# A fused scan and two expert layers on one core: tail clears, scatters, a page table and two ranks moved to other slots

## The chip, the core and the metric

The kernel runs on one core of a Trainium2 chip. The metric is the device time of one execution in microseconds; three runs of the kernel before took 588.43, 592.61 and 591.45 us, median 591.45. The profile is of one further execution.

## The reference

Three layers, in float32. The first is a gated linear scan over 4 batches, 8 heads and 768 positions, the second a dense layer pair with a leaky activation, the third a layer of 8 experts of which each token uses one:

```python
y[:, :, sl] = y_intra + y_inter                  # scan by chunks: (C B^T * decay) x + C state * decay
x = y.transpose(0, 2, 1, 3).reshape(3072, 256)
h = x @ w_in                                     # 256 -> 2048
x = (np.maximum(h, 0) + alpha * np.minimum(h, 0)) @ w_out
logits = x @ w_gate + modality_bias[modality_id] # 8 experts
e_idx = np.argmax(logits, axis=1)
for e in range(8):                               # each token goes to one expert
    mask = e_idx == e
    out[mask] = gate_w[mask, None] * (np.maximum(x[mask] @ w1[e], 0) @ w2[e])
```

## The kernel before, in words

**Blocks.** The 3072 tokens are 24 chunks of 128, grouped in nine blocks (`SIZES`: three of 2 chunks, six of 3). For each block the scan is computed, then the dense pair in 16 pieces of the hidden width. A piece is one *slot*: `unit_mm` multiplies into PSUM (`ph`), ScalarE and VectorE form the activation (`t`, `g`), `unit_split` splits it in a high part on ScalarE (`gh`) and a low part on GpSimd (`gl`, L618), and four slots later (`LAG`) `unit_g2` multiplies both by the second matrix into `px`. The scan of the next block runs in the same slots. Every matrix product is done in three matmuls on such high and low parts.

**Routing.** When a block is done, its tokens are routed: `route_mm` and `route_act` give the logits, `route_b` to `route_gate` the expert and its weight, `route_c` the ranks of the tokens within their expert (small matmuls into `pr`), `route_d` (L553) the row of each token in the DRAM buffer `srt`, and keeps the running count per expert in `cnt`. Still in `route_d`, one indirect DMA per chunk (L569), issued from GpSimd, scatters the 128 rows of the chunk to `srt`. In `srt` each expert has its own region, read later in pages of 256 rows.

**Clears.** An expert's last page is not full. `tail_counts` (L1012) copies `cnt` to integers (`cnti`, L1013), and `clear_tails` (L457) issues, from SyncE, one DMA per expert that writes 5 x 128 empty rows (645 KB) behind the counted ones. The rows of the last block are scattered after the clears, over them; the rows of the other blocks don't overlap them.

**Pages.** 14 pages of 256 rows follow, 8 slots each. For a page, SyncE reads the expert and the first row from a table (`item_tables`, computed on VectorE from `cnt` in five steps, one a slot: `sets`, `rk`, `knw`, `va`, `tab`). There are three: table 0 serves pages 0 and 1, table 1 pages 2 to 8, table 2 the rest. `item_load` (L771) loads 2 MB of the expert's weights in four DMAs (`raw`), `item_rows` (L786) the 256 rows (`xr`); the latter waits for all scatters and clears that stand before it in the program. `item_split` makes high and low weights on ScalarE and VectorE, `item_tr_mm` transposes the rows on TensorE (`pt`, L827), `item_tr_act` splits them (`x2h` on ScalarE, `x2l` on VectorE, L837); `item_g1` and `item_g2` are the two matmul steps (`rh`, `rl`).

**The order.** From block 3 on the order on each engine is written by hand: 96 block slots, numbered 0 to 95 (blocks 3 to 8), then 112 page slots. `do(u, fn, ...)` puts a step behind the work of slot `u`; `at[k, f]` is the slot of piece `f` of block `k`, so `at[8, 11]` is slot 91, and `ui` is slot 96. Within a slot the steps stand in the order of the `do` calls. Each engine takes its instructions in order. Block 7 is routed up to slot 90 and block 8 up to slot 106. Pages 0 and 1 are loaded at slots 83 and 84, page 2 at slot 96.

Of the kernel before, what the change touches and what calls it, by code (L numbers as in the profile page):

```python
# [112 lines left out]
def ssm_moe_moe_kernel(  # L113
# [26 lines left out]
    blocks = [(sum(SIZES[:k]), n) for k, n in enumerate(SIZES)]  # L140
# [57 lines left out]
    blk = {}  # L198
# [160 lines left out]
    m2p = []  # L359
# [187 lines left out]
    scat, tails = [], []  # L547

    def wait_for(i, o, why):
        tc.add_manual_dep(i, o.name, mybir.DependencyInfo(mybir.DependencyClass.Sync, mybir.DependencyReason.DATA),  # L550
                          reason=why)

    def route_d(k):  # L553
        c0, n = blocks[k]
        d = blk[k]
        pr, oh, xr = d["pr"], d["oh"], d["xr"]
        sh = [P, n, NE]
        V = nc.vector

        q = small.tile([P, MX, NE], F32, tag="q", name="q")  # L560
        V.tensor_tensor(q[:, :n], pr[:, :n], cnt[:, None, :].to_broadcast(sh), ALU.add)
        V.tensor_tensor(cnt, pr[:, n], cnt, ALU.add)
        V.tensor_tensor(q[:, :n], q[:, :n], oh[:, :n], ALU.mult)
        pf = small.tile([P, MX], F32, tag="pf", name="pf")
        V.tensor_reduce(pf[:, :n], q[:, :n], AX.X, ALU.add)
        pi = small.tile([P, MX], I32, tag="pi", name="pi")
        V.tensor_copy(pi[:, :n], pf[:, :n])
        for t in range(n):
            sc = nc.gpsimd.indirect_dma_start(  # L569
                out=srt[:, :], out_offset=bass.IndirectOffsetOnAxis(ap=pi[:, t:t + 1].bitcast(U32), axis=0),  # L570
                in_=xr[:, t, :ROW], in_offset=None, bounds_check=NROW - 1, oob_is_err=False)

            for o in scat:
                tc.declare_no_dep(sc.ins, o, reason="rows are disjoint")
            scat.append(sc.ins)
            if k == len(blocks) - 1:
                for o in tails:
                    wait_for(sc.ins, o, "rows behind the last ones")
# [366 lines left out]
                nk += 1  # L945
    for step in (route_a, route_b, route_exp, route_gate, route_c, route_d):
        step(0)

    last = len(blocks) - 1
    slots = [("m",) + q for q in late] + [("i", i, fc) for i in range(NSTATIC) for fc in range(KF2)]
    at = {q[1:]: u for u, q in reversed(list(enumerate(slots))) if q[0] == "m"}
    ui = len(late)
# [3 lines left out]
    def do(u, fn, *args):  # L958
        todo.setdefault(u, []).append((fn, args))
# [65 lines left out]
    def route_at(k, mms, b):  # L1025
        for t, u in enumerate(mms):
            do(u, route_mm, k, t)
            do(u + 1, route_act, k, t)
        for v, fn in zip(b, (route_b, route_exp, route_gate, route_c, route_d)):
            do(v, fn, k)  # L1030

    u = at[NS, 0]
    route_at(1, (u, u + 1), (u + 4, u + 5, u + 6, u + 6, u + 8))
    route_at(2, (u + 5, u + 7), (u + 9, u + 10, u + 11, u + 11, u + 14))
    for k in range(NS, last + 1):
        u = at[k, 15] + 1
        if k < last - 1:
# [4 lines left out]
    def table_at(u, j, pool):  # L1042
        steps = []

        def step():
            if not steps:
                steps.append(item_tables(j, pool[-1]))
            next(steps[0], None)

        for v in range(u, u + 5):  # L1050
            do(v, step)

    table_at(at[last - 1, 14], 0, small_)
    table_at(at[last, 11], 1, m2p)
    do(ui, tail_counts)
    table_at(ui + 12, 2, m2p)

    for k in range(NS, last):
        c0, n = blocks[k + 1]
# [3 lines left out]
        for j in range(n):  # L1063
            c, b = c0 + j, at[k, 0] + 5 * j - (k > NS)
# [29 lines left out]
    for i in range(2, NSTATIC):  # L1094
        b = ui + KF2 * (i - 2)
# [109 lines left out]
```

## Time and profile before

| what | before |
| --- | --- |
| runs, us | 588.43, 592.61, 591.45 |
| profiled execution, us | 591.03 |
| its span, us | 589.2 |
| mean granted clock of TensorE | 0.956 |
| TensorE busy, us | 555.0 (94%) |
| VectorE, ScalarE, GpSimd busy, us | 431.7, 314.6, 238.6 |

TensorE is the engine with the most work, and 34 us of the span are not busy. The span's first 150 us hold the conversion of the weights and blocks 0 to 2, the block slots 0 to 95 lie from there to about 401 us, the pages behind. All times in rows are microseconds from the start of the span. PEclk is the granted TensorE clock as a share of 2.4 GHz.

### The profile page before, as it was taken

To read this page: it belongs to the slowest core of one execution; us is meant where nothing else is said; L and a number is where in the kernel's file an instruction comes from. 1 tells how busy PE (TensorE), PEld (TensorE's weight loads), DVE (VectorE), ACT (ScalarE), POOL (GpSimd) and SP (SyncE) were. 2 spreads that over 40 slices of the span, in tenths; PEclk is the share of its full clock that TensorE was granted. 3 is DMA by queue.
4 is the path that set the end of the run, shared out by engine and by line. 5 is a ranking of instruction groups with operands and counts; after the bars stand their busy time and mean duration, and the time that the engine had idled before them with its cause. 6 is when DMAs were issued, how large, how long until landed. Compare 5 with 4: busy or idle time off the path is not lost. (4 is left out here: it accounts for less than half of the span.)

```text
span 589.2 us, 12123 instructions
## 1 busy us (share of the span) xinstructions
PE 555.0 (94%) x4303; PEld 519.4 (88%) x4303; DVE 431.7 (73%) x857; ACT 314.6 (53%) x696; POOL 238.6 (41%) x258
## 2 busy tenths in 40 slices
PE   7989989998999989999999999997969999999993
PEld 7877878898988878999999999997969999999993
DVE  4999999834677877777677777487568778777860
ACT  1346756755443553444444444573546677767751
POOL 1144345554545635845746646453022122111211
PEclk9695999999799999999999999997979999999998
DMA  7856654420127335224243200721998877776400
GB/s 247 270 188 197 191 180 136 135 81 10 44 89 213 121 116 171 90 101 137 84 138 113 71 12 27 260 91 62 288 330 279 279 224 227 227 234 217 154 18 6
DMA packets 59124, 89.27 MB, mean 152 GB/s; under 512 B 5071, under 2 KB 37009, under 8 KB 59057
## 3 DMA queue, kind: packets, MB, share of 16 engines
q1 hardware_dynamic: 55942, 80.73, 43.4%
q0 software_dynamic: 2400, 6.32, 3.0%
q10 hardware_dynamic: 714, 1.38, 0.9%
q8 instruction: 36, 0.59, 0.4%
q14 instruction: 32, 0.25, 0.1%
HBM read 73.50 MB, written 15.17 MB: 150 GB/s over the span
## 5 line engine op out<-in xcount | busy, mean ns | idle before, releaser
L618 POOL TENSOR_TENSOR gl<-g,gh 128x384 fp32r<-128x384 f32 (+1 forms) x144 | 145.5, 1014 | 140.3 <-ACT gh L616 139.9
L607 ACT ACTIVATE t<-ph,sgn 128x384 f32<-128x384 f32 (+1 forms) x144 | 78.5, 545 | 120.5 <-PE ph L153 113.8
L609 DVE SCALAR_TENSOR_TENSOR g<-ph,sal,t 128x384 f32<-128x384 f32 (+1 forms) x144 | 81.3, 565 | 76.8 <-ACT t L607 69.7
L153 PE MATMUL ph<-xh,wi_h 128*128 128x384 f32 (+1 forms) x288 | 99.1, 346 | 2.3 <-DVE g L609 2.1
L153 PE MATMUL px<-gl,wo_h 128*128 128x384 f32 (+1 forms) x288 | 94.4, 328 | 2.3 <-POOL gl L618 2.2
L153 PE MATMUL px<-gh,wo_h 128*128 128x384 f32 (+1 forms) x288 | 93.8, 326 | 0.2 <-ACT xT L646 0.2
L153 PE MATMUL px<-gh,wo_l 128*128 128x384 f32 (+1 forms) x288 | 93.4, 325 | 0.3 <-DVE wo_l L159 0.3
L153 PE MATMUL ph<-xl,wi_h 128*128 128x384 f32 (+1 forms) x288 | 92.6, 322 | 0.0
L153 PE MATMUL ph<-xh,wi_l 128*128 128x384 f32 (+1 forms) x288 | 92.7, 322 | 0.0
L616 ACT CAST gh<-g 128x384 fp32r<-128x384 f32 (+1 forms) x144 | 67.6, 471 | 18.1 <-DVE g L609 17.6
L876 POOL DMA_INDIRECT out_dram<-ob,xr x26 | 27.9, 1071 | 112.1 <-ACT ob L875 62.5
L853 ACT ACTIVATE rh<-ph 128x256 fp32r<-128x256 f32 (+1 forms) x112 | 41.5, 371 | 54.3 <-PE ph L153 54.0
L854 DVE SCALAR_TENSOR_TENSOR rl<-ph,rh 128x256 fp32r<-128x256 f32 (+1 forms) x112 | 45.1, 403 | 23.3 <-ACT rh L853 22.4
L153 PEld LDWEIGHTS ph<-xh,wi_h 128*128 128x128 f32 x288 | 55.1, 193 | 7.4 <-DVE g L609 3.3
L153 PEld LDWEIGHTS px<-gl,wo_h 128*128 128x128 f32 x288 | 55.8, 194 | 4.0 <-POOL gl L618 2.7
L153 PEld LDWEIGHTS px<-gh,wo_h 128*128 128x128 f32 x288 | 55.8, 194 | 1.0 <-ACT xT L646 0.5
L153 PEld LDWEIGHTS px<-gh,wo_l 128*128 128x128 f32 x288 | 55.8, 194 | 0.7 <-DVE wo_l L159 0.5
L153 PEld LDWEIGHTS ph<-xl,wi_h 128*128 128x128 f32 x288 | 55.3, 192 | 0.4 <-DVE xl L159 0.3
L153 PEld LDWEIGHTS ph<-xh,wi_l 128*128 128x128 f32 x288 | 55.2, 192 | 0.2 <-DVE g L609 0.2
L153 PE MATMUL ph<-x2h,wi_h 128*128 128x256 f32 x144 | 41.8, 290 | 4.4 <-DVE rl L854 4.4
L964 DVE TENSOR_TENSOR_SCAN ab<-ab,id 128x512 f32<-128x512 f32 x30 | 44.2, 1475 | 0.0
L569 POOL DMA_INDIRECT srt<-xr,pi x24 | 25.7, 1072 | 42.0 <-DMA raw<-in_w_dram 29.0
(149 smaller groups left out, 1306.4 us busy)
## 6 DMA issues: line engine op xcount, KB each, us to landing
raw<-in_w_dram SPq DMA_DIRECT2D x56, 512.0 KB
ab<-a_scr SPq DMA_DIRECT2D x24, 512.0 KB
srt<-zr SPq DMA_DIRECT2D x8, 645.0 KB
raw<-in_w_in_dram SPq DMA_DIRECT2D x8, 512.0 KB
raw<-in_w_out_dram SPq DMA_DIRECT2D x8, 512.0 KB
xr<-srt SPq DMA_DIRECT2D x14, 258.0 KB
bs<-bcs SPq DMA_DIRECT2D x30, 96.0 KB
bs<-bcs SPq DMA_DIRECT2D x15, 192.0 KB
```

Of the source, the lines that this page charges most:

```text
L153: nc.tensor.matmul(o, l, r, start=start, stop=stop)
L569: sc = nc.gpsimd.indirect_dma_start(out=srt[:, :], out_offset=bass.IndirectOffsetOnAxis(ap=pi[:, t:t + 1].bitcast(U32), axis=0), in_=xr[:, ...
L607: nc.scalar.activation(t[:, :N], ph[:, :N], AF.Copy, scale=sg)
L609: nc.vector.scalar_tensor_tensor(g[:, :N], ph[:, :N], sal[:, fc:fc + 1], t[:, :N], ALU.mult, ALU.max)
L616: nc.scalar.copy(gh[:, :N], g[:, :N])
L618: nc.gpsimd.tensor_tensor(gl[:, :N], g[:, :N], f(gh[:, :N]), ALU.subtract)
L853: nc.scalar.activation(rh[:, :n], ph[:, :n], AF.Relu)
L854: nc.vector.scalar_tensor_tensor(rl[:, :n], ph[:, :n], 0.0, f(rh[:, :n]), ALU.max, ALU.subtract)
L876: nc.gpsimd.indirect_dma_start(out=out[:, :], out_offset=bass.IndirectOffsetOnAxis(ap=xr[:, t, ROW - 1:ROW].bitcast(U32), axis=0), in_=ob, ...
L964: nc.vector.tensor_tensor_scan(lt[:, s_].rearrange("p h i -> p (h i)"), lt[:, s_].rearrange("p h i -> p (h i)"), id8[:, s_].rearrange("p h ...
```

## The change

Five things move, and no computation is added or taken away. The scatters leave `route_d` and become a step of their own, `route_out`; for blocks 1 to 7 one chunk is scattered in each of the slots behind `route_d`, where two or three stood together. A scatter of a block before the last no longer depends on the clears, wherever it stands. The clears go from slot 96 to slot 91. Table 1 goes from slots 91 to 95 to slots 93 to 97. For blocks 1 and 2 the ranks (`route_c`) and `route_d` come one slot later.

```diff
--- before.py
+++ after.py
@@ -553,7 +553,7 @@
     def route_d(k):
         c0, n = blocks[k]
         d = blk[k]
-        pr, oh, xr = d["pr"], d["oh"], d["xr"]
+        pr, oh = d["pr"], d["oh"]
         sh = [P, n, NE]
         V = nc.vector
 
@@ -565,12 +565,16 @@
         V.tensor_reduce(pf[:, :n], q[:, :n], AX.X, ALU.add)
         pi = small.tile([P, MX], I32, tag="pi", name="pi")
         V.tensor_copy(pi[:, :n], pf[:, :n])
-        for t in range(n):
+        d["pi"] = pi
+
+    def route_out(k, ts):
+        pi, xr = blk[k]["pi"], blk[k]["xr"]
+        for t in ts:
             sc = nc.gpsimd.indirect_dma_start(
                 out=srt[:, :], out_offset=bass.IndirectOffsetOnAxis(ap=pi[:, t:t + 1].bitcast(U32), axis=0),
                 in_=xr[:, t, :ROW], in_offset=None, bounds_check=NROW - 1, oob_is_err=False)
 
-            for o in scat:
+            for o in scat + (tails if k < len(blocks) - 1 else []):
                 tc.declare_no_dep(sc.ins, o, reason="rows are disjoint")
             scat.append(sc.ins)
             if k == len(blocks) - 1:
@@ -945,6 +949,7 @@
                 nk += 1
     for step in (route_a, route_b, route_exp, route_gate, route_c, route_d):
         step(0)
+    route_out(0, range(blocks[0][1]))
 
 
 
@@ -1029,9 +1034,16 @@
         for v, fn in zip(b, (route_b, route_exp, route_gate, route_c, route_d)):
             do(v, fn, k)
 
+        n = blocks[k][1]
+        if k < last:
+            for t in range(n):
+                do(b[-1] + 1 + t, route_out, k, (t,))
+        else:
+            do(b[-1], route_out, k, range(n))
+
     u = at[NS, 0]
-    route_at(1, (u, u + 1), (u + 4, u + 5, u + 6, u + 6, u + 8))
-    route_at(2, (u + 5, u + 7), (u + 9, u + 10, u + 11, u + 11, u + 14))
+    route_at(1, (u, u + 1), (u + 4, u + 5, u + 6, u + 7, u + 9))
+    route_at(2, (u + 5, u + 7), (u + 9, u + 10, u + 11, u + 12, u + 15))
     for k in range(NS, last + 1):
         u = at[k, 15] + 1
         if k < last - 1:
@@ -1051,8 +1063,8 @@
             do(v, step)
 
     table_at(at[last - 1, 14], 0, small_)
-    table_at(at[last, 11], 1, m2p)
-    do(ui, tail_counts)
+    table_at(at[last, 13], 1, m2p)
+    do(at[last, 11], tail_counts)
     table_at(ui + 12, 2, m2p)
 
     for k in range(NS, last):
```

How the order on the engines moves is seen at two places. The first is VectorE at the end of the block slots. Before: `sets`, `rk`, `knw`, `va`, `tab` are table 1, `w2l` and `wi_l` the weights of pages 0 and 1, `x2l` page 0's rows, `rl` page 0's first slot.

```order
L734 TENSOR_TENSOR knw<-knw,rk 128x96
L159 TENSOR_TENSOR w2l<-raw_4982,w2h 128x512
L609 SCALAR_TENSOR_TENSOR g<-ph,sal,t 128x384
L737 SCALAR_TENSOR_TENSOR va<-rk,cst 128x192
L740 TENSOR_REDUCE tf<-va 128x2
L741 CAST tab_168<-tf 128x2
L837 TENSOR_TENSOR x2l<-pt,x2h 128x512
L609 SCALAR_TENSOR_TENSOR g<-ph,sal,t 128x384
L159 TENSOR_TENSOR wi_l<-raw_5032,wi_h 128x2x256
L854 SCALAR_TENSOR_TENSOR rl<-ph_5385,rh 128x256
L1013 CAST cnti<-cnt 128x8
```

The same place in the change, from the multiplication of `rk` in table 1 on:

```order
L728 TENSOR_TENSOR rk<-rk,sets 128x288
L731 TENSOR_TENSOR rk<-rk 128x96 x2
L841 TENSOR_TENSOR x2l<-pt,x2h 128x512
L613 SCALAR_TENSOR_TENSOR g<-ph,sal,t 128x384
L735 TENSOR_SCALAR knw<-rk 128x96
L737 TENSOR_SCALAR rk<-rk 128x96
L738 TENSOR_TENSOR knw<-knw,rk 128x96
L159 TENSOR_TENSOR wi_l<-raw_5032,wi_h 128x2x256
L858 SCALAR_TENSOR_TENSOR rl<-ph_5461,rh 128x256
L741 SCALAR_TENSOR_TENSOR va<-rk,cst 128x192
L744 TENSOR_REDUCE tf<-va 128x2
L745 CAST tab_168<-tf 128x2
```

And in the change a little earlier on VectorE, where the count of the clears stands now:

```order
L613 SCALAR_TENSOR_TENSOR g<-ph,sal,t 128x384
L1018 CAST cnti<-cnt 128x8
L159 TENSOR_TENSOR w2l<-raw_4980,w2h 128x512
L613 SCALAR_TENSOR_TENSOR g<-ph,sal,t 128x384
L159 TENSOR_TENSOR w2l<-raw_4982,w2h 128x512
L613 SCALAR_TENSOR_TENSOR g<-ph,sal,t 128x384
L698 SCALAR_TENSOR_TENSOR sets<-cnt,cst 128x96 x2
```

`cnti` stood behind the first `rl` of the pages and now stands five slots earlier, ahead of the table; the table's last three operations stood ahead of `x2l` and now stand behind the first `rl`.

The second place is GpSimd in the same slots, where the scatters of blocks 7 and 8 are issued. Before, block 7's, then block 8's:

```order
L618 TENSOR_TENSOR gl<-g,gh 128x384 x13
L569 DMA srt<-xr,pi 26880x258 x3
L618 TENSOR_TENSOR gl<-g,gh 128x384 x6
L569 DMA srt<-xr,pi 26880x258 x3
L876 DMA out_dram<-ob,xr_4984 3072x256 x2
```

In the change:

```order
L573 DMA srt<-xr,pi 26880x258
L622 TENSOR_TENSOR gl<-g,gh 128x384
L573 DMA srt<-xr,pi 26880x258
L622 TENSOR_TENSOR gl<-g,gh 128x384
L573 DMA srt<-xr,pi 26880x258
L622 TENSOR_TENSOR gl<-g,gh 128x384 x3
L573 DMA srt<-xr,pi 26880x258 x3
```

Block 7's three scatters have a `gl` between each two; block 8's three still stand together. On SyncE the sequence stays the same: eight clears, then page 2's weights and rows.

## Rows read from the trace of the kernel before

**Rows 1.** Waits of TensorE, whole run: us in total, times, longest.

```profile
PE ph L153 <- DVE rl L854: 4.4, 1, 4.4
...
PE ph L153 <- DVE x2l L837: 2.5, 1, 2.5
```

**Rows 2.** Stretches: us, busy PE, PEld, DVE, ACT, POOL (instructions), PEclk, DMA share, GB/s.

```profile
210.00:220.00 10.00, 7.88 (x47) 7.12 (x46) 7.27 (x13) 5.78 (x11) 3.46 (x4) 1.00 0.38 108
...
390.00:400.00 10.00, 10.00 (x68) 9.96 (x66) 9.69 (x21) 5.69 (x12) 7.38 (x7) 1.00 0.12 41
...
405.40:410.50 5.10, 5.06 (x19) 5.07 (x20) 2.69 (x5) 1.64 (x5) 1.01 (x1) 0.50 0.15 51
...
433.40:437.70 4.30, 3.64 (x16) 3.38 (x17) 4.13 (x17) 2.98 (x8) 0.00 (x0) 0.50 1.07 371
...
460.00:570.00 110.00, 110.00 (x939) 110.00 (x939) 85.29 (x161) 78.28 (x181) 22.51 (x21) 1.00 0.64 199
```

**Rows 3.** Timeline of TensorE, first gap: start, us, instruction, [idle before, releaser].

```profile
402.58 0.39 PE L153 MATMUL ph<-x2h,w1h 128*128 128x256 f32 x1 [1.23 <-ACT x2h L836]
...
405.44 0.58 PE L153 MATMUL ph<-x2l,w1h 128*128 128x256 f32 x1 [2.47 <-DVE x2l L837]
...
406.46 0.41 PE L153 MATMUL ph<-x2h,w1l 128*128 128x256 f32 x1
...
406.67 0.52 PE L153 MATMUL px<-gh,wo_h 128*128 128x384 f32 x1
...
411.90 0.28 PE L153 MATMUL ph<-x2h,w1l 128*128 128x256 f32 x1
...
412.01 0.34 PE L153 MATMUL px<-gh,wo_h 128*128 128x384 f32 x1
```

**Rows 4.** Timeline of VectorE around the first gap, and table 2.

```profile
392.71 0.61 DVE L609 SCALAR_TENSOR_TENSOR g<-ph,sal,t 128x384 f32<-128x384 f32 x1
...
396.07 3.71 DVE L724 TENSOR_TENSOR rk<-rk,sets 128x288 f32<-128x288 f32 x1
...
403.07 0.63 DVE L737 SCALAR_TENSOR_TENSOR va<-rk,cst 128x192 f32<-128x192 f32 x1
...
404.70 0.68 DVE L837 TENSOR_TENSOR x2l<-pt,x2h 128x512 fp32r<-128x512 f32 x1
...
407.73 0.17 DVE L1013 CAST cnti<-cnt 128x8 int32<-128x8 f32 x1
...
441.80 0.35 DVE L724 TENSOR_TENSOR rk<-rk,sets 128x192 f32<-128x192 f32 x1
```

**Rows 5.** Timeline of GpSimd: one undisturbed subtraction, then block 7's scatters and the pile.

```profile
371.95 1.02 POOL L618 TENSOR_TENSOR gl<-g,gh 128x384 fp32r<-128x384 f32 x1 [1.10 <-ACT gh L616]
...
392.47 1.19 POOL L569 DMA_INDIRECT srt<-xr,pi  x1 [1.29 <-DVE pi L567]
...
396.49 2.96 POOL L618 TENSOR_TENSOR gl<-g,gh 128x384 fp32r<-128x384 f32 x3
```

**Rows 6.** Timeline of TensorE, second gap, and the transposes of page 3.

```profile
433.49 0.58 PE L153 MATMUL ph<-x2h,wi_h 128*128 128x256 f32 x1 [4.43 <-DVE rl L854]
...
436.99 1.09 PE L827 MATMUL pt<-cst,xr 128*128 128x128 f32 x4 [0.57 <-DMA xr<-srt]
...
449.23 0.60 PE L827 MATMUL pt<-cst,xr 128*128 128x128 f32 x4
```

**Rows 7.** Timeline of ScalarE: the wait for page 2's weights.

```profile
431.75 0.62 ACT L815 CAST wi_h<-raw 128x512 fp32r<-128x512 f32 x1 [6.34 <-DMA raw<-in_w_dram]
```

**Rows 8.** Timeline of SyncE's issues: clears, weights of page 2, rows of pages 2, 3.

```profile
408.78 12.76 SPq L461 DMA_DIRECT2D srt<-zr  x8
...
423.06 2.92 SPq L783 DMA_DIRECT2D raw<-in_w_dram  x4
...
430.59 0.38 SPq L790 DMA_DIRECT2D xr<-srt  x1
...
443.77 0.38 SPq L790 DMA_DIRECT2D xr<-srt  x1
```

## The prediction

> **What bounds the kernel now.** I read the list of TensorE's waits first [rows 1]. The largest two of the late part are a wait of 4.4 us for `rl` and one of 2.5 us for `x2l`; both lie where the last block hands over to the expert pages. Then busy time and granted clock by stretches [rows 2]: TensorE is 10.00 of 10 busy at 1.00 in the block stage (390 to 400) and 110.00 of 110 in the page stage (460 to 570). A microsecond of TensorE's own work is therefore a microsecond of the kernel, and so is a gap of it; other engines matter where they make a gap. Two stretches stand out, 405.4 to 410.5 and 433.4 to 437.7, both at a granted clock of 0.50, the lower level (1.2 GHz), and each follows a gap.
>
> *First gap* [rows 3]. After the last block's matmuls TensorE idles 1.23 us for `x2h` and 2.47 us for `x2l`, and then runs at the lower clock: two 256-column matmuls start 0.21 us apart (406.46, 406.67), later 0.11 us (411.90, 412.01). Why is `x2l` late? VectorE [rows 4] spends 3.71 us (396.07) on one multiplication of 128x288 for table 1, where the same line took 0.35 us on 128x192 in table 2 (441.80). In just that time GpSimd [rows 5] runs three `gl` subtractions in one go (396.49, 2.96 us). They came in one go because the three scatters of block 7's rows, the first at 392.47, stood ahead of them in its queue until the pile began. So three scatters in a row piled up three `gl`, the pile held VectorE, and everything behind it there was late, `x2l` last.
>
> *Second gap* [rows 6]. TensorE idles 4.43 us at 433.49 and 0.57 us at 436.99 for page 2's gathered rows. ScalarE's row [rows 7] names the cause: it sat 6.34 us, until 431.75, for page 2's weights, and being in order could not produce the `rh` that TensorE needed. SyncE [rows 8] shows why they were late: eight tail clears (645 KB each) are issued from 408.78 for 12.76 us, and only then, at 423.06, the weights.
>
> **Part by part.** The sum is made against the profiled execution's own 591.03 us (span 589.2 and 1.8 around it); the median of the runs, 591.45, is 0.4 above.
>
> *Tails at slot 91 instead of 96.* `cnti` ran at 407.73 and the first clear 1.05 us later. In the new order `cnti` stands right behind the `g` that starts at 392.71 and lasts 0.6, so it runs at about 393.3 and the first clear goes at 394.4: 14.4 us earlier. The eight clears are then issued by 407.2. The transfer engines are nearly empty there (0.12 busy, 41 GB/s from 390 to 400 [rows 2]), and no weights are in flight, so nothing that TensorE waits for is delayed. Page 2's weights follow on SyncE: they were issued 14.3 us after the first clear, so now at 408.7, and were there 23.0 us after it, so now at 417.4. ScalarE wanted them 6.34 us before 431.75, at 425.4; with the first gap gone it wants them at about 420.2. That leaves 2.8 us of slack, and the second gap goes. The gathered rows of page 2, issued 21.8 us after the first clear (430.59), go at 416.2 and are wanted at about 425.3 instead of 436.99.
>
> *Table 1 two slots later.* SyncE needs it for page 2's load. Its last three operations took from 403.07 to 404.70 and now stand behind `x2l` and the first `rl` of page 0; I put its end at about 405.5. SyncE is busy with clears until 407.2, so the table is 1.7 us early and this delay costs nothing. If the clears did not cover it, a later table would move the weights by as much.
>
> *Scatters one a slot.* The same 24 scatters of some 1.2 us stay on GpSimd; none is added. Undisturbed, GpSimd works 1.02 us on a `gl` and idles 1.10 before it (371.95 [rows 5]), so a slot of the block stage is some 2.1 us: one scatter and one `gl` fill it, and no pile of three forms. This lets block 7's scatter run free beside the clears, too. What does `x2l` gain? It started at 404.70. Ahead of it disappear about 3.3 us of held multiplication (3.71 less some 0.45, scaled from the 0.35) and 1.63 us of the table; `cnti` adds under 0.2. By VectorE's work alone it could start at 399.9 and be done 0.7 us later. From the other side: three single `gl`, each holding one operation of VectorE for its whole 1.0 us, put its start at 402.9 and its end at 403.6. TensorE wants it at about 401.3, since 402.58 less 1.23 is when it was free. The remaining gap is thus 0 to 2.3 us. I take 0.8: nearer the free end, because the other end needs all three to meet. Gaps of that size need not cost the clock: from 210 to 220 TensorE was busy 7.88 of 10, in several short gaps, and was granted 1.00 throughout [rows 2].
>
> The row at 396.07 shows VectorE held while GpSimd computes. The Trainium skill ("SBUF — State Buffer", section "SBUF: two separate sides") says that a VectorE operation with two SBUF inputs and a GpSimd operation exclude one another for a whole instruction, whichever starts first. By that rule spreading doesn't remove the exclusion, it only makes each meeting one `gl` long, and the sum would move toward the upper end above; the trace agrees with it in that 3.71 us end just behind the third `gl`.
>
> *Ranks of blocks 1 and 2 one slot later.* The same instructions, one slot on, in a stretch for which the list of TensorE's waits has no long one. Nothing waits for the scatters of those blocks before page 0, 200 us later. I take 0 and bound it by one `gl`, 1.0 us, either way.
>
> *What is late next.* Page 3's rows wait for block 8's scatters. They were issued at 443.77 [rows 8] and wanted at 449.23 [rows 6], 5.5 us on. Those scatters need the ranks (TensorE's time, 5.2 us earlier) and page 2's rows (14.4 us earlier), so I expect the issue at about 431 for a use at 437.6: just covered.
>
> *The sum.* First gap: 1.23 + 2.47 idle, and 5.06 us of work at half clock [rows 2] that takes about 0.55 of it at full (0.11 to 0.12 us against 0.21): 2.3. Together 6.0; less 0.8 left: 5.2. Second gap: 4.43 + 0.57 idle, and 3.64 us at half clock, worth 1.6: 6.6. Total 11.8, so 591.0 - 11.8 = 579.2; with the median's 0.4 about 579.5.
>
> **The rivals.**
>
> *The lock moves rather than goes* (0.13). Each `gl` meets another of VectorE's operations and `x2l` ends at its upper bound. The gap of 2.3 us is close to the 2.47 after which the clock fell, so it may also cost 2.3 of clock: 11.8 + 0.8 - 4.6 = 8.0 gained, 583.0. For it: the hold of 3.71 us shows that VectorE's operation and GpSimd's do not overlap, and the same number of `gl` must run. Against: `x2l` reads PSUM, and its own 0.68 us shows no hold.
>
> *The clears go early but the weights don't* (0.11): the change does not do what it says. SyncE takes page 2's load only after table 1; the weights need 8.7 us from issue to use (423.06 to 431.75) and TensorE felt 1.9 us less than ScalarE (4.43 against 6.34), so an issue behind 420.2 + 1.9 - 8.7 = 413.4 opens the gap again. If VectorE is so far behind with the table, the weights are late and the second gap stays whole or in large part. Only the first goes: 591.0 - 5.2 = 585.8. Against: `x2l`, the operation ahead, would itself have to be 7 us late.
>
> *Slower: more meetings in every block* (0.04). In blocks 3 to 7, 15 scatters now push a `gl` each into other places of VectorE's order, among the attention scans. If in each of five blocks one held operation makes a gap of 2.5 us, from which on the clock falls, each costs 2.5 + 2.3: 24 us, and 591.0 - 11.8 + 24 = 603. Below that gap nothing follows, since TensorE is 10.00 busy there with the pile of three in place, which speaks against it.
>
> *Forecast as above* (0.72): its own range 577.5 to 581.5.
>
> **Numbers.** A change under 1% of the median cannot be told from none here: 585.5 to 597.4. Faster by over 1%: the forecast and the first rival, 0.72 + 0.13, less 0.01 for the upper edge: 0.84. Within: the second rival and that edge, 0.12. Slower 0.04. The range: downward the whole 12.6 gives 578.4, and the runs shown reach 3 us under their median, so 577.0; upward it takes in the first rival with 2 us for its unknown gap, 585.0. What lies outside is most of the second rival and the last.
>
> **What would show it.** In the profile after: (1) the multiplication of 128x288 under 1.5 us, and GpSimd alternating scatter and `gl`; (2) the first clear within 2 us of 394.4, the weights' issue near 409; (3) no wait of ScalarE for page 2's weights and no clock of 0.50 between 400 and 440; (4) a gap before page 0's second matmul under 1.3 us; (5) span about 577 to 578. I am wrong if a wait for `xr` or `raw` appears at pages 2 or 3, or if `x2l` still ends after 403.6.

## The result and the profile after

The changed kernel took 582.96 us (median of 4 runs, 581.59 to 584.12) against 590.81 us (4 runs, 588.43 to 592.61): ratio 0.9862, 95% interval 0.9835 to 0.9889, so 1.4% faster. The profiled execution took 582.98 us, its span 581.2 us at a mean clock of 0.967. The forecast was 579.5 us and the range 577.0 to 585.0. The time lies in the range, but only two thirds of the 11.8 us of the sum came, and the rows show which.

**The second gap is gone.** SyncE's issues in the changed kernel (start, duration, count), the rows that answer to [rows 8]: clears, weights of page 2, rows of pages 2 and 3.

```profile
394.70 12.83 SPq L461 DMA_DIRECT2D srt<-zr  x8
409.84 4.27 SPq L787 DMA_DIRECT2D raw<-in_w_dram  x4
418.82 0.38 SPq L794 DMA_DIRECT2D xr<-srt  x1
...
434.97 0.38 SPq L794 DMA_DIRECT2D xr<-srt  x1
```

The clears start 14.1 us earlier, the weights 13.2 us. On ScalarE the conversion that waited 6.34 us [rows 7] now starts without a wait for page 2's weights, since its row carries no idle time:

```profile
424.21 0.63 ACT L819 CAST wi_h<-raw 128x512 fp32r<-128x512 f32 x1
```

**The first gap stays.** TensorE's timeline there, against [rows 3]: `x2h` is ready in time now, `x2l` is not, and all the idle time is in one piece of 3.55 us (1.23 + 2.47 before). Behind it three 384-column matmuls stand 0.32 us apart, at the lower clock. The last row is page 2's transposes, 436.99 before [rows 6].

```profile
401.30 0.28 PE L153 MATMUL ph<-x2h,w1h 128*128 128x256 f32 x1
405.14 0.38 PE L153 MATMUL ph<-x2l,w1h 128*128 128x256 f32 x1 [3.55 <-DVE x2l L841]
...
406.08 0.52 PE L153 MATMUL px<-gh,wo_l 128*128 128x384 f32 x1
406.40 0.52 PE L153 MATMUL px<-gl,wo_h 128*128 128x384 f32 x1
406.72 0.52 PE L153 MATMUL px<-gh,wo_h 128*128 128x384 f32 x1
...
429.21 0.60 PE L831 MATMUL pt<-cst,xr 128*128 128x128 f32 x4
```

The same in stretches (columns as in [rows 2]): 3.8 us all but idle, 3.3 us at a granted clock of 0.50, the lower level of 1.2 GHz, then 1.00 through the place of the old second gap and through the pages.

```profile
401.30:405.10 3.80, 0.28 (x2) 0.02 (x1) 3.73 (x8) 1.03 (x2) 0.99 (x1) 1.00 1.08 273
405.90:409.20 3.30, 3.30 (x14) 3.30 (x14) 3.23 (x7) 1.30 (x3) 1.01 (x1) 0.50 1.09 268
409.20:433.00 23.80, 23.42 (x196) 23.15 (x196) 17.29 (x55) 15.01 (x37) 3.17 (x4) 1.00 0.93 275
460.00:570.00 110.00, 110.00 (x939) 110.00 (x939) 82.32 (x159) 75.77 (x177) 22.40 (x20) 1.00 0.59 182
```

GpSimd (against [rows 5]) does alternate scatter and `gl`, as the change wants:

```profile
395.31 1.02 POOL L622 TENSOR_TENSOR gl<-g,gh 128x384 fp32r<-128x384 f32 x1
396.50 1.25 POOL L573 DMA_INDIRECT srt<-xr,pi  x1 [0.17 <-issue]
397.77 1.02 POOL L622 TENSOR_TENSOR gl<-g,gh 128x384 fp32r<-128x384 f32 x1
398.97 0.99 POOL L573 DMA_INDIRECT srt<-xr,pi  x1 [0.17 <-issue]
399.99 1.03 POOL L622 TENSOR_TENSOR gl<-g,gh 128x384 fp32r<-128x384 f32 x1
403.38 0.99 POOL L622 TENSOR_TENSOR gl<-g,gh 128x384 fp32r<-128x384 f32 x1 [2.36 <-ACT gh L620]
```

And VectorE (against [rows 4]) in the same time. An operation is called held here where it takes longer than the same line takes when no `gl` runs beside it:

```profile
393.36 0.46 DVE L1018 CAST cnti<-cnt 128x8 int32<-128x8 f32 x1
...
395.30 1.58 DVE L159 TENSOR_TENSOR w2l<-raw,w2h 128x512 fp32r<-128x512 f32 x1 [0.23 <-ACT w2h L819]
...
397.33 1.76 DVE L698 SCALAR_TENSOR_TENSOR sets<-cnt,cst 128x96 f32<-128x96 f32 x2
...
399.71 1.93 DVE L719 TENSOR_TENSOR_SCAN rk<-cst,sets 128x288 f32<-128x288 f32 x1
...
402.68 0.44 DVE L728 TENSOR_TENSOR rk<-rk,sets 128x288 f32<-128x288 f32 x1
403.15 1.33 DVE L731 TENSOR_TENSOR rk<-rk 128x96 f32<-128x96 f32 x2
404.40 0.68 DVE L841 TENSOR_TENSOR x2l<-pt,x2h 128x512 fp32r<-128x512 f32 x1
```

The multiplication of 128x288 that took 3.71 us takes 0.44. But the three operations around it, and one weight split, each end 0.1 to 0.6 us behind a `gl`: `w2l` 1.58 us, `sets` 1.76, the scan 1.93, the additions to `rk` 1.33. In the kernel before the same lines took 0.68, 0.42, 0.76 and 0.55; `sets` and the scan stood there beside block 7's scatters, and the last operation of the table, `tab`, was held by the `gl` of 403.77 to 404.76:

```profile
393.24 0.42 DVE L694 SCALAR_TENSOR_TENSOR sets<-cnt,cst 128x96 f32<-128x96 f32 x2
...
394.28 0.76 DVE L715 TENSOR_TENSOR_SCAN rk<-cst,sets 128x288 f32<-128x288 f32 x1
...
404.12 0.68 DVE L741 CAST tab<-tf 128x2 int32<-128x2 f32 x1
```

```profile
393.96 0.98 POOL L569 DMA_INDIRECT srt<-xr,pi  x1 [0.30 <-issue]
```

With 0.29 on `cnti` (0.46 against 0.17 before) VectorE is held 4.5 us in five pieces ahead of `x2l`, where it was held some 3.3 on the multiplication and 0.5 on `tab` (0.17 unheld, in gl_on_vector). `x2l` starts at 404.40, 0.3 us earlier than before.

**A new wait, early.** At 194 us TensorE waits 1.13 us for an `xl`, which it did not before. It is made in block 3's last slot, as an input of block 4's first product. VectorE, then TensorE:

```profile
191.96 0.62 DVE L613 SCALAR_TENSOR_TENSOR g<-ph,sal,t 128x384 f32<-128x384 f32 x1 [3.03 <-ACT t L611]
192.49 0.17 DVE L561 TENSOR_TENSOR q<-pr,cnt 128x16 f32<-128x16 f32 x1
...
193.60 0.17 DVE L567 CAST pi<-pf 128x2 int32<-128x2 f32 x1
193.68 0.42 DVE L159 TENSOR_TENSOR xl<-py,xh 128x256 fp32r<-128x256 f32 x1
```

```profile
194.16 0.44 PE L153 MATMUL ph<-xl,wi_h 128*128 128x384 f32 x1 [1.13 <-DVE xl L159]
```

Block 2's `route_d` (192.49 to 193.77) now stands between a `g` and the `xl` that TensorE wants.

**The ledger.** Marks that every kernel has, from the starts of rows: the g of VectorE, 144 in all, 16 a block (the 63rd stands in slot 14, the 75th in slot 26, so between them lie the end of block 3 and most of block 4), and the four transposes `pt` that open a page. Span 589.2 to 581.2, in us:

| stretch | before | after | difference |
| --- | --- | --- | --- |
| up to the 63rd g | 189.15 | 188.31 | -0.84 |
| 63rd to 75th g (ranks of block 2) | 37.53 | 38.68 | +1.15 |
| 75th g to slot 91's g | 166.03 | 165.84 | -0.19 |
| page 0's `pt` to page 1's (first gap) | 16.49 | 15.25 | -1.24 |
| page 1's to page 2's (second gap) | 23.93 | 17.27 | -6.66 |
| page 2's to page 3's | 12.24 | 12.04 | -0.20 |

The rest differs by under 0.05. The first line is no work of the change: at the 51st g (157 us), ahead of the first moved step, this execution already lies 0.85 us ahead of before, and those of the kernels below lie between -1.3 and +1.3 us. Their early stretches at the lower clock differ from one execution to the next.

### The profile page after: what moved, and what is told of

Read it like the earlier page. It is cut to its first block, busy times and chain, and to the rows that moved or that the text cites. A ratio compares the mean times of both kernels' runs of the same rounds, so it can differ in the third digit from the quotient of the medians.

```text
span 581.2 us, 12122 instructions
## 1 busy us (share of the span) xinstructions
PE 552.0 (95%) x4303; PEld 516.9 (89%) x4303; DVE 434.1 (75%) x857; ACT 315.0 (54%) x696; POOL 238.9 (41%) x258
## 5 line engine op out<-in xcount | busy, mean ns | idle before, releaser
L622 POOL TENSOR_TENSOR gl<-g,gh 128x384 fp32r<-128x384 f32 (+1 forms) x144 | 143.0, 994 | 147.6 <-ACT gh L620 147.1
L880 POOL DMA_INDIRECT out_dram<-ob,xr x26 | 29.3, 1126 | 112.0 <-ACT ob L879 55.4
L153 PE MATMUL ph<-x2l,wi_h 128*128 128x256 f32 x144 | 40.4, 280 | 0.0
```

Of the source, the lines that this page charges most:

```text
L153: nc.tensor.matmul(o, l, r, start=start, stop=stop)
L622: nc.gpsimd.tensor_tensor(gl[:, :N], g[:, :N], f(gh[:, :N]), ALU.subtract)
L880: nc.gpsimd.indirect_dma_start(out=out[:, :], out_offset=bass.IndirectOffsetOnAxis(ap=xr[:, t, ROW - 1:ROW].bitcast(U32), axis=0), in_=ob, ...
```

## The experiments

Three sets, each with its own runs of the kernel before (medians 590.8, 593.09 and 591.71); ratios go to those, and intervals are 95%. The table has the ledger's stretches for all of them, in us:

| kernel | time | ratio | 63rd-75th g | page 0-1 | page 1-2 |
| --- | --- | --- | --- | --- | --- |
| before (profile) | 591.03 | 1 | 37.53 | 16.49 | 23.93 |
| clears_only | 583.71 | 0.9891 (0.9856-0.9926) | 37.56 | 16.75 | 17.28 |
| clears_back | 592.90 | 1.0036 (1.0013-1.0059) | 38.65 | 15.21 | 27.05 |
| scatters_together | 585.69 | 0.9914 (0.9888-0.9940) | 38.64 | 16.02 | 17.27 |
| table_back | 582.55 | 0.9863 (0.9822-0.9905) | 38.67 | 13.04 | 17.25 |
| table_behind | 581.45 | 0.9794 (0.9771-0.9817) | 38.69 | 9.90 | 20.12 |
| gl_on_vector | 580.28 | 0.9785 (0.9766-0.9804) | 38.67 | 11.05 | 18.53 |
| ranks_back | 583.93 | 0.9852 (0.9831-0.9872) | 37.53 | 16.26 | 17.28 |
| table_behind_ranks_back | 581.10 | 0.9799 (0.9781-0.9817) | 37.56 | 9.91 | 19.82 |
| after_again | 583.63 | 0.9873 (0.9843-0.9902) | 38.65 | 15.27 | 17.27 |
| table_back_again | 583.02 | 0.9842 (0.9805-0.9879) | 38.70 | 13.02 | 19.22 |
| table_back_ranks_back | 581.87 | 0.9839 (0.9806-0.9872) | 37.54 | 14.37 | 17.63 |
| gl_on_vector_ranks_back | 580.17 | 0.9811 (0.9779-0.9843) | 37.55 | 11.07 | 17.43 |

**The clears alone, and all but the clears.** The first is the kernel before with this edit, the second the changed kernel with its reverse:

```diff
-    do(ui, tail_counts)
+    do(at[last, 11], tail_counts)
```

> The kernel before with one edit: the tail clears at slot 91. Theory A (GpSimd's `gl` hold VectorE's table operations; the clears have nothing to do with it): the second gap goes, the first stays as it was before (1.2 + 2.5 us and half clock), so 6.6 us under before, about 584.2. Theory B (the transfers of the clears, now beside the table, slow VectorE's operations): the first gap grows by 2 to 4 us, 586 to 588.

> The changed kernel with the clears back at slot 96, all else as changed. Theory A: table 1's `sets` and scan are held as in the changed kernel (1.8 and 1.9 us), the first gap stays near 3.6 us and the second gap of about 4.4 us is back: some 6.6 us above the changed kernel, 589.6. Theory B: with no clears beside them the same operations take 0.4 and 0.8 us, the first gap falls under 1 us, and the total is about 585.

The clears alone give 7.1 us of the change's 7.9 and the whole of the second gap (17.28). Without them the change is 0.4% slower than before: `cnti` stands behind the later table (410.68), the clears start at 411.73, 0.8 us later against slot 91's g than before, the weights are there 24.1 us behind the first clear instead of 23.0, and page 1 comes 1.3 us sooner. So the wait is longer, 9.45 us on ScalarE and 7.54 on TensorE (6.34 and 4.43 in [rows 6, 7]):

```profile
435.79 0.62 ACT L819 CAST wi_h<-raw 128x512 fp32r<-128x512 f32 x1 [9.45 <-DMA raw<-in_w_dram]
```

```profile
437.52 0.58 PE L153 MATMUL ph<-x2h,wi_h 128*128 128x256 f32 x1 [7.54 <-DVE rl L858]
```

In clears_only both the loss of the second gap and the first gap (16.75 against 16.49) came as theory A said, so the clears' transfers beside the table cost VectorE nothing there. In clears_back the first gap stayed, as theory A said, but the time went 3.3 us past it.

**The scatters in one slot again**, the rest as changed:

```diff
-                do(b[-1] + 1 + t, route_out, k, (t,))
+                do(b[-1], route_out, k, (t,))
```

> The changed kernel with the scatters of a block in one slot again (each block's two or three right behind its ranks), all else as changed. Theory A: three `gl` in one go again hold one operation of VectorE for about 3 us, the others are free; the sum of the holds is the same, the first gap stays at 2.5 to 4.5 us, and the time within 1.5 us of 583.0. If spreading were what gained the time: 585 or more.

2.7 us more than the changed kernel in time, which is past the 1.5 of theory A and in the range that was to mean that spreading gains something. The page 0-1 stretch has 0.8 of it, with a wait for `x2l` of 4.4 us. The profiled span is 2.4 us longer, but 1.6 of that lies ahead of the 51st g, so where the rest of the 2.7 comes from is not shown. GpSimd first, then VectorE: a pile of four `gl`, and `sets` stuck in it.

```profile
398.57 3.94 POOL L622 TENSOR_TENSOR gl<-g,gh 128x384 fp32r<-128x384 f32 x4
```

```profile
400.18 2.62 DVE L698 SCALAR_TENSOR_TENSOR sets<-cnt,cst 128x96 f32<-128x96 f32 x2
```

**The table where it was**, the rest as changed, in two sets:

```diff
-    table_at(at[last, 13], 1, m2p)
+    table_at(at[last, 11], 1, m2p)
```

> The changed kernel with table 1 back at slot 91, all else as changed. Theory A: the operations of the table's last steps stand ahead of `x2l` again (2.2 us of work, and they can be held too), the gap before page 0's second matmul grows from 3.6 to 5 to 7 us, the time to 585 to 587. If the table's place does not matter: 583.0 and a gap of 3.6 us.

> The changed kernel once more, so that the others of this call stand beside it on one chip. Both theories expect what it showed before: 0.986 of the time before (0.9835 to 0.9889), one wait for x2l of about 3.5 us and then some 3.4 us at a granted clock of 0.50, no second gap.

> Table 1 at slots 91 to 95 as before, the rest as in the change. Its first profile showed a wait for x2l of 2.67 us instead of 3.55 and no stretch at 0.50 behind it, against 3.4 us at 0.50 in the change. Theory A (moving the table two slots later costs): 0.9 us of gap and 1.7 us of clock less than the changed kernel, so 2 to 3 us faster than it in the same call. Theory B (the table's place is worth nothing, as the two medians of the first call say): within 1 us of the changed kernel, and a half-clock stretch behind the gap in this profile.

The first expectation (slower) fell. after_again showed the changed kernel's stretches once more. VectorE of table_back, then GpSimd: the scan starts beside a scatter and is not held (0.76 us); the `gl` that follows the scatter is (1.30 us).

```profile
396.45 0.76 DVE L719 TENSOR_TENSOR_SCAN rk<-cst,sets 128x288 f32<-128x288 f32 x1
397.12 0.93 DVE L1018 CAST cnti<-cnt 128x8 int32<-128x8 f32 x1
```

```profile
396.71 1.30 POOL L622 TENSOR_TENSOR gl<-g,gh 128x384 fp32r<-128x384 f32 x1
```

Its gap is 2.67 us instead of 3.55, no stretch behind it lies under a clock of 1.00, and page 1 comes 2.2 us sooner (13.0 against 15.3, the same in both sets). So moving the table cost 2.2 us at the first gap in these executions. Of that 0.9 is idle time, which every execution shows, and the rest is clock, which not every one does: table_back_ranks_back has the same order here, was at 0.50 for 3.4 us, and took 14.37. The time hardly shows the move (582.55 against 582.96, and 583.02 against 583.63 in one set, within the 1 us of theory B, though without theory B's stretch at half clock), and table_back_again's profile shows one reason: with the table at slot 91 its first operations stand ahead of `cnti`, the clears start 4.4 us behind slot 91's g instead of 1.9, and page 2's rows are late. SyncE, then a line of TensorE's waits:

```profile
398.28 12.65 SPq L461 DMA_DIRECT2D srt<-zr  x8
412.07 6.26 SPq L787 DMA_DIRECT2D raw<-in_w_dram  x4
423.09 0.38 SPq L794 DMA_DIRECT2D xr<-srt  x1
```

```profile
PE pt L831 <- DMA xr<-srt: 1.8, 1, 1.8
```

In table_back's own profile the clears are as late (4.4 us) and yet the rows came in time; the two executions differ there by 2 us, and why is not shown.

**The table behind `x2l`**, with page 2's load two slots later:

```diff
-    table_at(at[last, 13], 1, m2p)
+    table_at(at[last, 15], 1, m2p)
-        do(b, item_load, i, 1 if i >= NFULL else 2)
-        do(b if i == 2 else b + 6, item_rows, i)
+        do(b + 2 if i == 2 else b, item_load, i, 1 if i >= NFULL else 2)
+        do(b + 2 if i == 2 else b + 6, item_rows, i)
```

> The changed kernel with table 1 in slots 95 to 99, so behind `x2l` on VectorE, and page 2's load two slots later, since it reads that table. Theory A: no held operation stands ahead of `x2l` any more, the first gap falls from 3.6 us to under 0.8 and the half clock behind it goes: 4 to 4.5 us under the changed kernel, about 578.6. Page 2's weights are then issued near 411 and wanted by ScalarE near 420, which is tight: up to 2 us may be lost to them. If `x2l` is late for another reason (ScalarE, the `g` ahead): no gain, 583.

> The changed kernel with both: table 1 behind `x2l` and the ranks of blocks 1 and 2 as before. If both explanations hold, the gains add: 4 to 5.5 us under the changed kernel, about 577.8.

The first gap is gone (9.90 us from page 0 to page 1, no wait for `x2l` there), 5.4 us of it. Then page 1-2 is 2.9 us longer: TensorE waits 1.46 us for page 1's `x2l`, which now stands behind the table (0.38 in the changed kernel), and for page 2's rows:

```profile
428.13 0.63 PE L831 MATMUL pt<-cst,xr 128*128 128x128 f32 x4 [1.63 <-DMA xr<-srt]
```

So the next limit lies 2 to 3 us behind the first gap, and by the stretches half of the gain is given back there. Both kernels missed the times expected, 578.6 and 577.8, by some 3 us; their set holds no run of the changed kernel, and their ratios, 0.7% below its own, leave room for more than the 2.5 us that the stretches show.

**The `gl` of block 8's slots 10 to 14 on VectorE**, the rest as changed; the second kernel has the old ranks too:

```diff
-        nc.gpsimd.tensor_tensor(gl[:, :N], g[:, :N], f(gh[:, :N]), ALU.subtract)
+        low = nc.vector if k == len(SIZES) - 1 and 10 <= fc <= 14 else nc.gpsimd
+        low.tensor_tensor(gl[:, :N], g[:, :N], f(gh[:, :N]), ALU.subtract)
```

> The changed kernel with the low parts (`gl`) of block 8's pieces 10 to 14 computed on VectorE, so that GpSimd has only scatters beside table 1. Theory A: the table's operations are no longer held (`sets` 0.4 us for two, scan 0.8 us), and VectorE has about 0.5 us more for each of the three or four `gl` ahead of `x2l` and waits for ScalarE's half: the gap is 1 to 2.5 us, the time 580.5 to 582.5. If the operations are slow for another reason: `sets` 1.8 and scan 1.9 us remain, and the gap grows to 5 us or more, 585.

> The gl subtractions of the last block's slots 10 to 14 on VectorE, and the ranks of blocks 1 and 2 as before; the rest as in the change. Theory A (what remains of the first gap is gl holding VectorE's operations, and the rank step costs 1.1 us by itself): x2l waits under 1 us, no clock of 0.50 between 400 and 440, and 4.5 us faster than the changed kernel in the same call, 0.977 to 0.979 of the time before. Theory B (page 2's rows already bound it, so an earlier start is given back there): the wait for xr at page 2 grows by as much from its 1.1 us, and the time stays 3.4 us below the changed kernel.

VectorE has 5 x 0.55 us more to do, and is done sooner. In the second kernel:

```profile
398.10 0.42 DVE L699 SCALAR_TENSOR_TENSOR sets<-cnt,cst 128x96 f32<-128x96 f32 x2
...
399.13 0.76 DVE L720 TENSOR_TENSOR_SCAN rk<-cst,sets 128x288 f32<-128x288 f32 x1
...
401.87 0.55 DVE L732 TENSOR_TENSOR rk<-rk 128x96 f32<-128x96 f32 x2
402.34 0.68 DVE L842 TENSOR_TENSOR x2l<-pt,x2h 128x512 fp32r<-128x512 f32 x1
```

```profile
403.08 0.39 PE L153 MATMUL ph<-x2l,w1h 128*128 128x256 f32 x1 [0.90 <-DVE x2l L842]
```

No operation is held, the gap is 0.90 us (1 to 2.5 was expected), and the clock stays:

```profile
400.00:412.00 12.00, 11.10 (x76) 10.73 (x75) 9.77 (x24) 7.20 (x17) 1.06 (x1) 1.00 1.10 267
```

From page 0 to page 2 it takes 28.50 us against 40.42 before: 11.9 less, where the forecast's sum was 11.8; that the two agree is chance, since this kernel has other steps than the forecast's. Its time is 580.17 us, 3.5 below the changed kernel in the same set; 4.5 was expected if both savings add in full, 3.4 if page 2's rows took the ranks' part, and in its profile those rows cost no wait. The stretches support the first; the time is the second's, so the two together don't decide it. gl_on_vector, with the new ranks, did wait for page 2's rows, 1.1 us, so that limit lies close.

**The ranks as before**, alone and with the table back:

```diff
-    route_at(1, (u, u + 1), (u + 4, u + 5, u + 6, u + 7, u + 9))
-    route_at(2, (u + 5, u + 7), (u + 9, u + 10, u + 11, u + 12, u + 15))
+    route_at(1, (u, u + 1), (u + 4, u + 5, u + 6, u + 6, u + 8))
+    route_at(2, (u + 5, u + 7), (u + 9, u + 10, u + 11, u + 11, u + 14))
```

> The changed kernel with the ranks of blocks 1 and 2 in the slots of before. The changed kernel shows TensorE waiting 1.1 us at 194.2 for block 3's `xl`, behind block 2's ranks on VectorE, which before did not. If the slot of the ranks makes it: this wait goes, 0.5 to 1.2 us under the changed kernel, about 582. If it comes from the scatters' new places: it stays, 583.

> Only the spread scatters and the early clears; table 1 and the ranks of blocks 1 and 2 stand as before. Theory A (the ranks' move costs 1.1 us at block 3, whatever else changes): 1.1 us faster than table_back_again, no wait of TensorE for xl between 185 and 200, and if the table's move costs as well, 3 to 4 us faster than the changed kernel. Theory B (the rank step is noise): equal to table_back_again within 0.5 us.

The wait for `xl` is gone, and VectorE has `route_d` ahead of the g again:

```profile
191.13 0.17 DVE L567 CAST pi<-pf 128x2 int32<-128x2 f32 x1
193.13 0.62 DVE L613 SCALAR_TENSOR_TENSOR g<-ph,sal,t 128x384 f32<-128x384 f32 x1 [1.83 <-ACT t L611]
193.74 0.42 DVE L159 TENSOR_TENSOR xl<-py,xh 128x256 fp32r<-128x256 f32 x1
```

From the 63rd to the 75th g it takes 37.53 to 37.56 us in the six executions with the old ranks and 38.64 to 38.70 in the eight with the new, so the step costs 1.1 us. In table_back_ranks_back it shows in the time as expected (581.87 against 583.02), though the two intervals overlap. In ranks_back it does not: there the same 3.56 us wait for `x2l` was followed by a longer stretch at the lower clock (0.59 from 405 to 412, 0.76 in the changed kernel), and page 0-1 took 1.0 us more.

**What spreading does by itself.** table_back_ranks_back and clears_only differ in the places of the scatters alone: both have the clears at slot 91, the table and the ranks where they were. With the scatters together (clears_only) the multiplication is held to 3.73 us and TensorE idles 1.32 and 2.48 us; with one scatter a slot the multiplication takes 0.44 and the idle time is 2.67. The wait in clears_only, then in table_back_ranks_back:

```profile
404.63 0.58 PE L153 MATMUL ph<-x2l,w1h 128*128 128x256 f32 x1 [2.48 <-DVE x2l L837]
```

```profile
403.35 0.58 PE L153 MATMUL ph<-x2l,w1h 128*128 128x256 f32 x1 [2.67 <-DVE x2l L841]
```

VectorE is held 2.6 us ahead of `x2l` in the second, 3.8 in the first, and page 0-1 takes 14.37 us against 16.75 (13.04 in table_back). So with the table in its old place spreading is worth 2.4 to 3.7 us at the first gap; with the table two slots later it is worth 0.8 (scatters_together). Much of what the scatters gained there the table's move took back. The times (ratios 0.9839 and 0.9891) lean the same way, with intervals that overlap.

## Why the prediction was right in sign and range, and 3.5 us too low

- **Clears at slot 91: right, in its time and its size.** First clear 394.4 foretold, 394.70 measured; weights 408.7 and 409.84; second gap 6.6 us foretold, 6.66 measured. The chain clears, weights, `rh` is shown by clears_only and clears_back. Page 3's rows were covered, as foretold, though issued at 434.97 instead of 431: no wait, 12.04 us from page 2 to 3.
- **"The remaining gap is thus 0 to 2.3 us. I take 0.8 ... because the other end needs all three to meet": this step failed.** 3.55 us remained, above the upper end. The step counted the three `gl` of the old pile. Between slot 91's g and `x2l` four single `gl` now run, a fifth holds `cnti`, and all five meet something. The 399.9 that VectorE's work alone allowed and 4.5 us of holds make 404.4, where `x2l` started: 0.3 us sooner instead of 2 to 5. (Two smaller terms about cancel: `knw`, 0.5 us, also went behind `x2l` and was left out, and VectorE idles some 0.3.) The sum's 5.2 us became 1.24, of which 0.15 is idle time and some 0.8 clock: 3.3 us of work at the lower one instead of 5.06, at 0.45 each; the remaining 0.3 is not placed.
- **"This delay costs nothing", said of table 1: also wrong, at a place I did not look at.** I priced its end, which SyncE waits for, and not its beginning. Before, `sets` and the scan ran beside block 7's scatters, unheld; two slots later they stand where the single `gl` are. table_back shows 2.2 us for it, 0.9 of them idle time; with the table in its old place the same spread scatters held VectorE 2.6 us ahead of `x2l` instead of 4.5. What it saves, 2.5 us for the clears, since `cnti` now comes ahead of the table, I had put down to the clears' move alone.
- **The ranks: 0 within 1.0 foretold, +1.1 measured.** "A stretch for which the list of TensorE's waits has no long one" was true and beside the point: the row to read was the slack of the next `xl` on VectorE's queue, and there was none.
- **The rival "the lock moves rather than goes" is what happened**, at 583.0 foretold and 582.96 measured. Its price came right by luck, out of two errors: the gap was 1.2 us longer than it said, the clock cost 0.8 or 0.9 less than it charged, and the ranks' 1.1 us and the faster start (0.8) nearly cancel. I had held against it that `x2l` reads PSUM; that was no reason, since the holds are in what stands ahead of `x2l`.
- Of the five signs, the multiplication, the clears and ScalarE came as said; the clock (0.50 from 405.9 to 409.2), the gap and the span did not, and `x2l` ends at 405.1, behind the 403.6 that I had named as the point of error.

That a running `gl` is what holds VectorE is shown by the kernels that move it: with the `gl` on VectorE the same `sets`, scan and additions take 0.42, 0.76 and 0.55 us, and in the kernel before `sets` and the scan took 0.42 and 0.76 while scatters ran. The Trainium skill ("SBUF — State Buffer", section "SBUF: two separate sides") says that a VectorE operation with two SBUF inputs and a GpSimd operation that reads SBUF exclude one another for a whole instruction. By that rule spreading leaves the exclusion in place, and the trace of the changed kernel agrees: 4.5 us held in five pieces against 3.8 in two. (`cnti` and `tab`, which have one input, were held too, 0.46 and 0.68 us against 0.17; this sentence does not cover them.) How much is held still depends on what stands where, as the 2.6 us of table_back_ranks_back show.

## What to carry to other kernels

When a pile on one engine holds another, count every instruction of the holder between the mark and the use, not those of the pile: spreading them changes where they meet, and the total can shrink (3.8 to 2.6 us with the table in its old place) or grow (to 4.5 with the table moved as well). A moved step has to be priced at its first instruction as well as its last, by what it now stands beside and what queue order it changes. To get rid of the meetings, move the holder's work to the held engine or the held work behind the use, and then ask what is late next: here that limit lay 2 to 3 us on.

## What was not expected of the hardware

- **The same gap, with and without a price in clock.** A wait of 2.66 to 2.67 us for `x2l` was followed by no stretch under 1.00 in table_back and table_back_again, and accompanied by 3.4 us at 0.50 in table_back_ranks_back. Waits of 3.5 to 3.6 us brought 3.4 us at 0.50 in three executions and 6.8 in ranks_back, and the 4.4 us of scatters_together no more than 3.4. So the prediction's "a gap of 2.5 us, from which on the clock falls", taken from one gap, did not hold as a rule. For one code path that is 13.0 or 14.4 us from page 0 to page 1, for another 15.2 or 16.3, so one profile does not size such a gap better than to 1 us or somewhat more.
- **A recorded start doesn't tell who holds whom.** In the changed kernel the scan is recorded 0.28 us ahead of a `gl` (399.71 and 399.99), and the scan grew (1.93 us, the `gl` 1.03). In table_back it is recorded 0.26 ahead (396.45 and 396.71), and the `gl` grew (1.30, the scan 0.76). The page of the Trainium skill named above says, in the same section, that whichever starts first has the shared pair of ports for the whole instruction; the recorded starts fit that in table_back and not in the changed kernel, and which of the two truly began first no run shows.
